# One loop over four chunks of 128 channels for the long convolution, three chunks returned through memory

## The chip, the cores and the metric

The kernel runs on one core of one Trainium2 chip. The metric is device time in microseconds of one execution; the kernel before is given by the median of three runs. A core has five engines that run their own instruction streams: TensorE (PE in the profile; its weight loads are shown apart as PEld), VectorE (DVE), ScalarE (ACT), GpSimd (POOL) and SyncE (SP). Here SP does nothing but issue transfers between the chip's memory (DRAM) and the on-chip memory.

## What is computed

A block with adaptive layer norms around two parts, for 2048 tokens of 512 channels, all in float32:

```python
mod = (silu(c) @ w_mod).reshape(6, 512)          # sa, ca, ga, sb, cb, gb
h = layernorm(q) * (1 + ca) + sa
k_shift = causal 4-tap convolution of k, per channel
kv = k_shift * v
y = causal convolution of kv with ssm_k over all 2048 tokens, per channel (by FFT)
y = y + kv * ssm_D
x = q + ga * (h * y)
h = layernorm(x) * (1 + cb) + sb
out = x + gb * ((silu(h @ w_gate) * (h @ w_up)) @ w_down)     # 512 -> 1792 -> 512
```

The kernel does the long convolution by a transform in two steps, written as matrix products: a first step of length 64 (`e_fwd`), an exchange of two axes, a second step of length 32 (`w_c`), a product with the transformed filter, and the same backwards. `ssm_D` is added to the first filter tap, so it needs no pass of its own.

## The kernel before, in words

Every engine call goes through the class `InOrder` (lines 32 to 41), which keeps each engine's instructions in the order in which the program issues them. So all rows of the profile name its line, L40, and are told apart by the tiles they write and read. Waits between engines and the places of tiles are set by the framework: a tile that asks for a place in a full pool waits until an older tile of that pool has been read for the last time.

**Places.** On-chip tiles come from pools by size: `b32` (32 KB per partition, 3 of them), `b16` (16 KB, 1), `e8` (8 KB, 9), `r4` (4 KB, 4), `k2` (2 KB, 3). Matrix products land in four pairs of PSUM banks (`banks`, line 67), handed out in turn.

**Preparing a chunk of 128 channels.** `load_k`, `load_v` and `load_ssm` bring k, v and the filter. `tap0` (line 102) and three `tap` (110) make the short convolution u on DVE (`tap0` of some chunks on ACT), `times_v` (116) multiplies by v. For the data, `trans` (146) turns four blocks of 128 x 128 for two chunks at a time on PE (tile kvt) and copies them on ACT, and `step1` (132) does the first transform step (tile s, 256 columns) with an ACT copy into X; `x1t` (157) runs both for two chunks and issues the next `trans` ahead of the two `step1`. For the filter, `skip` (512) adds `ssm_D` on DVE, `k1_step` (181) does the first step (tile s) and `k1_turn` (199) turns the result (tile kt) into K. X and K hold two chunks, 256 channels, and there are two of each (halves).

**The pieces.** The second step runs over pieces of 32 channels, 8 to a half, 16 in all. `swap` (173) exchanges the two axes of one piece of X by a 32 x 32 block transpose on DVE, in place. `k2nd(n)` (231) transforms the filter twice (`W2`, `W2S`, tile pk) and copies both results to ks on ACT; `x2nd(n)` (237) transforms the data (tile px) and multiplies px with both halves of ks on DVE, giving two R; `inv(n)` (248) turns R back (tile iv) and copies into X on ACT. `loop` (265) orders them: in step n the filter of piece n+1, the data of piece n, the swap of piece n+2, then the hooks of key `n`, `inv(n-1)`, the hooks of key `(n,)` and, in the second loop, the swap back of piece n-2.

**The order around them.** Both chunks of half 0 are prepared first (lines 516 to 562). `loop(0, 8)` (570) has the preparation of half 1's filter and u in its hooks, loads of `w_mod` (`mod_load`, 287) and the first of their products (`mod_bc`, 292, tile pb). Then comes `x1t(1)` and two more `mod_bc`. X0 isn't swapped back on DVE: `put` (210) writes it to memory, 1 KB at a time in the return by `get` (214), which reads it with the two axes exchanged, 32 partitions per transfer. The loads of the tokens (`load_x`) and of `e_inv` stand around it on SP. `loop(8, 16)` (624) has in its hooks `mod_T` (301, tile pm), the layer norm's statistics (`do_stats`, 607: DVE, with a small power on POOL), and the gates (`do_gate`, 610: two DVE and two ACT operations that scale x, then two POOL multiplications of 128 x 2048). Its last steps begin the backward first step, `y_piece` (363, tile y), which DVE multiplies into the gate S1 and `add_y` (382) adds to x.

**The entry to the feed-forward** (lines 635 to 671): the last two swaps, the split of the first weights into two parts (`split_w`, 435), the rest of y, the second layer norm of the first 512 tokens (`norm2a`, `norm2b`, `norm2c`: statistics, scale, turn on PE, split into two parts). From line 673 on `gate_up` (453, tile gu) and `down` (477, tile dn) run over 7 groups of weights and 4 groups of tokens, with three products for each float32 product.

Of the kernel before, what the change touches and what calls it, by code (L numbers as in the profile page):

```python
# [16 lines left out]
P = 128  # L17
# [26 lines left out]
def adaln_h3_swiglu(ctx, tc, q, kT, vT, shk, ssm, dskip, wgu, wdn, c, wmod, e_fwd, e_inv, w_c, out):  # L44
# [87 lines left out]
    def step1(j0, x, dst):  # L132


        ps = banks("s1")
        for jj in range(2):
            for a in range(2):
                pe.matmul(
                    ps[:, a, jj * H : (jj + 1) * H], raw[rows(a), j0 + jj], x[rows(a), jj, :], start=True, stop=True
                )  # L140
        act.copy(
            dst.rearrange("p (a j) d -> p a j d", a=2)[:, :, j0 : j0 + 2, :],
            ps.rearrange("p a (j d) -> p a j d", j=2),
        )

    def trans(h, jc):

        pt = banks("kvt")
        ptv = pt.rearrange("p a (j d) -> p (a j) d", j=2)
        for jj in range(4):  # L150
            for bb in range(2):
                pe.transpose(ptv[:, jj, bb * P : (bb + 1) * P], U[2 * h + bb][:, 4 * jc + jj :: J], ident)
        x = r4([P, 4, H], F32, f"x{h}_{jc}")
        act.copy(x, ptv)
        return x

    def x1t(h, nxt, hooks={}):
        dst = b32(f"X{h}")
        for jc in range(J // 4):
            x = nxt  # L160
            if jc + 1 < J // 4:
                nxt = trans(h, jc + 1)
            for o in range(0, 4, 2):
                step1(4 * jc + o, x[:, o : o + 2], dst)
            for f in hooks.get(jc, ()):
                f()
        return dst
# [10 lines left out]

    KT = {}

    def k1_step(h, i, jq):

        if (h, i) not in KT:
            KT[h, i] = b16(f"kt{h}{i}", (P, 4, 32, 32))
        ps = banks("s1")
        for jj in range(4):
# [72 lines left out]
    def swap_x(n):  # L259
        swap(seq[n][1], seq[n][2])  # L260
# [503 lines left out]
```

## Time and profile before

| | |
|---|---|
| runs of the kernel before | 731.72, 731.82, 733.17 us; median 731.82 |
| the profiled execution's own time | 731.3 us |
| its span, first to last instruction | 729.5 us, 8402 instructions |
| mean granted clock of TensorE | 0.954 |
| memory read and written | 40.51 and 8.39 MB |
| first product of the feed-forward (tile gu) | starts at 249.83 us |
| second step's first R, end of the last swap | 57.31 and 231.12 us |

A row of the busy times by stage gives a stretch of the span in us, its length, and for each engine its busy time in it with the number of instructions; then the granted clock of TensorE as a part of full speed, the mean busy share of the 16 transfer queues, and what they moved. The chain of waits follows the work that ended last back from the end: each row has a start, a length, an engine and the tile written; "issue" is time in which the engine waited for nothing that the profile shows. A row of the groups gives what is written and read, shapes, count, total and mean time, and the engine's idle time before it. In the list of transfers the last number is the time from issue to landing. Names without numbers stand for all tiles of that name.

### The profile page before, as it was taken

The numbers are of one execution on the slowest core, as the hardware profiler recorded it, in microseconds if no ns is written. First come the engines' busy times: TensorE is split into PE (matmuls) and PEld (weight loads), VectorE is DVE, ScalarE is ACT, GpSimd is POOL, SyncE is SP. The second block draws the span as 40 slices with busy tenths as digits, with TensorE's granted clock in tenths as the row PEclk, the third lists the DMA queues.
The fourth block names the chain that finished last, engine by engine and source line by source line (L and its number), as shares of the span: only waits on it lengthen the run. The fifth ranks groups of instructions, "written<-read, shape, count | busy, mean of one in ns | idle before, by whom it ended". The sixth has DMA issues, their size and how long they took to land.

```text
span 729.5 us, 8402 instructions
## 1 busy us (share of the span) xinstructions
PE 658.2 (90%) x3584; PEld 497.1 (68%) x3584; DVE 376.7 (52%) x476; ACT 232.9 (32%) x310; POOL 71.8 (10%) x36
## 2 busy tenths in 40 slices
PE   4499689997657679999999999999999999999997
PEld 4474345652114558888888888888888888888885
DVE  5619953269999678553334334343434433442333
ACT  3597535635312336521122112111112112211110
POOL 0000000004982353000000000000000000000000
PEclk9799989997888889999999999999999999999999
DMA  8613216996002000220000010000000000000113
GB/s 311 273 58 115 64 56 230 381 238 132 1 0 88 30 0 30 64 81 1 30 29 30 1 31 29 27 29 30 29 1 30 29 1 1 0 1 0 58 58 115
DMA packets 18150, 49.43 MB, mean 68 GB/s; under 512 B 1857, under 2 KB 6081, under 8 KB 16322
## 3 DMA queue, kind: packets, MB, share of 16 engines
q1 hardware_dynamic: 18114, 48.91, 20.2%
q8 instruction: 28, 0.46, 0.3%
q14 instruction: 8, 0.07, 0.0%
HBM read 40.51 MB, written 8.39 MB: 67 GB/s over the span
## 4 chain that ended last, share of the span: by engine, by line
PE 76%; DVE 14%; ACT 2%; DMA 2%; issue 2%; POOL 1%; SPq 0%; DVEq 0%; POOLq 0%; ACTq 0%
PE gu L40 40%; PE dn L40 21%; DVE X L40 4%; PE s L40 3%; DVE R L40 3%; PE pk L40 2%; DMA kt<-in_kT 2%; PE pb L40 2%; PE iv L40 2%; DVE s L40 1%; POOL s L40 1%; PE nt L40 1%; PE px L40 1%; PE kt L40 1%; PE kvt L40 1%
## 5 line engine op out<-in xcount | busy, mean ns | idle before, releaser
L40 PE MATMUL gu<-h,wg 128*128 128x512 f32 x1344 | 316.2, 391 | 0.4 <-DVE h L40 0.4
L40 PEld LDWEIGHTS gu<-h,wg 128*128 128x128 f32 x1344 | 253.3, 189 | 53.4 <-DVE h L40 0.8
L40 DVE TENSOR_TENSOR sg<-sg,gu 128x512 f32<-128x512 f32 x56 | 38.5, 688 | 216.7 <-ACT sg L40 216.7
L40 PE MATMUL dn<-wdb,h 128*128 128x512 f32 x576 | 138.0, 389 | 0.0
L40 ACT ACTIVATE sg<-gu 128x512 f32<-128x512 f32 x56 | 33.5, 599 | 289.2 <-PE gu L40 289.2
L40 PEld LDWEIGHTS dn<-wdb,h 128*128 128x128 f32 x576 | 108.1, 188 | 22.5
L40 DVE TENSOR_TENSOR x<-x,dn 128x512 f32<-128x512 f32 x112 | 71.9, 684 | 2.9 <-PE dn L40 2.9
L40 DVE STREAM_TRANSPOSE X<-X 128x1024 f32<-128x1024 f32 x24 | 53.5, 2249 | 36.5 <-ACT X L40 36.5
L40 DVE TENSOR_TENSOR h<-sg,h 128x512 fp32r<-128x512 f32 x56 | 38.7, 692 | 34.4 <-ACT h L40 34.4
L40 DVE TENSOR_TENSOR R<-px,ks 128x1024 f32<-128x1024 f32 x32 | 37.5, 1213 | 25.3 <-PE px L40 15.6
L40 ACT CAST h<-sg 128x512 fp32r<-128x512 f32 x56 | 34.8, 621 | 37.7 <-DVE sg L40 37.7
L40 PE MATMUL s<-er,ss 64*128 64x128 f32 x256 | 22.6, 344 | 25.5 <-issue 15.2
L40 PE MATMUL iv<-R,wc 64*64 64x512 f32 x256 | 36.7, 676 | 7.1 <-DVE R L40 3.7
L40 PE MATMUL pk<-K,wc 64*64 64x512 f32 x256 | 35.3, 675 | 7.8 <-DVE R L40 7.8
L40 PEld LDWEIGHTS s<-er,ss 64*128 64x128 f32 x256 | 20.9, 250 | 29.6 <-issue 17.0
L40 ACT COPY ks<-pk 128x1024 f32<-128x1024 f32 x32 | 31.1, 1022 | 24.4 <-PE pk L40 11.8
L40 POOL TENSOR_TENSOR s<-s,bcs 128x2048 f32<-128x2048 f32 x8 | 36.7, 4586 | 1.2 <-DVE s L40 0.9
L40 PEld LDWEIGHTS iv<-R,wc 64*64 64x64 f32 x256 | 11.3, 153 | 30.7 <-issue 23.0
L40 PE MATMUL px<-X,wc 64*64 64x512 f32 x128 | 21.0, 730 | 9.8 <-DVE R L40 9.7
L40 DVE SCALAR_TENSOR_TENSOR u<-kt,shk_sb,u 128x2047 f32<-128x2047 f32 (+2 forms) x12 | 27.9, 2327 | 2.6 <-ACT u L40 2.4
L40 ACT COPY X<-iv 128x1024 f32<-128x1024 f32 x16 | 16.2, 1010 | 32.7 <-PE iv L40 32.7
L40 PEld LDWEIGHTS pk<-K,wc 64*64 64x64 f32 x256 | 9.5, 145 | 24.2 <-issue 22.2
(68 smaller groups left out, 488.6 us busy)
## 6 DMA issues: line engine op xcount, KB each, us to landing
ws<-in_wgu SPq DMA_DIRECT2D x14, 512.0 KB, 3.3
wm<-in_wmod SPq DMA_DIRECT2D x6, 1024.0 KB, 7.7
ss<-in_ssm SPq DMA_DIRECT2D x8, 512.0 KB, 7.7
kt<-in_kT SPq DMA_DIRECT2D x4, 1024.0 KB, 7.9
vt<-in_vT SPq DMA_DIRECT2D x4, 1024.0 KB, 10.6
X<-X SPq DMA_DIRECT2D x1, 4096.0 KB, 12.4
x<-in_q SPq DMA_DIRECT2D x4, 1024.0 KB, 15.1
X<-X SPq DMA_DIRECT2D x4, 1024.0 KB, 21.4
```

Of the source, the lines that this page charges most:

```text
L40: return lambda *a, **k: self.tc.keep_in_program_order(f(*a, **k))
```

## The change

X and K now hold one chunk of 128 channels each (four of each), and one loop of 16 pieces runs over all four chunks, four pieces to a chunk. Only chunk 0 and u of chunk 1 are prepared before it. The rest of the preparation (`x_first`, `k_first`, `k_turn` and the taps, always one or two chunks ahead), the loads, the products with `w_mod`, the statistics and the gates stand in its hooks. Within a piece, the data's transform is now copied to xs (ACT), one piece ahead, and the filter's two transforms are multiplied straight out of PSUM (`product`), so that there are 16 copies of xs in place of 32 of ks. Chunks 0 to 2 go to memory and come back with the axes exchanged, in runs of 128 channels (512 bytes); chunk 3's four pieces are swapped back on DVE. The pools change: `b16` has 7 places and takes over what `b32` held, `e8` goes from 9 to 8, `r4` from 4 to 7. `load_k(0)` becomes the first large load. In the entry, `norm2b(0)` is issued before `add_y(1)`, `add_y(0)` is one operation, and `split_w(0, 2)` moves behind the first `gate_up`; the part of `w_down` for group 0 now shares its tile with the others.

```diff
-    def b32(name, shape=(P, 32, H), dt=F32):
-        return wp.tile(list(shape), dt, tag="b32", name=name, bufs=3)
-
-    def b16(name, shape, dt=F32):
-        return wp.tile(list(shape), dt, tag="b16", name=name, bufs=1)
+    def b16(name, shape=(P, 32, P), dt=F32):
+        return wp.tile(list(shape), dt, tag="b16", name=name, bufs=7)
...
-        return wp.tile(shape, dt, tag="e8", name=name, bufs=9)
+        return wp.tile(shape, dt, tag="e8", name=name, bufs=8)
...
-        return wp.tile(shape, dt, tag="r4", name=name, bufs=4)
+        return wp.tile(shape, dt, tag="r4", name=name, bufs=7)
...
+    def x_first(c_, half):
+        if half == 0:
+            X.append(b16(f"X{c_}"))
+        pt = banks("kvt").rearrange("p a (j d) -> p (a j) d", j=4)
+        for jj in range(8):
+            pe.transpose(pt[:, jj], U[c_][:, 8 * half + jj :: J], ident)
+        x = r4([P, 8, P], F32, f"x{c_}{half}")
+        act.copy(x, pt)
+        for o in range(0, 8, 4):
+            ps = banks("s1")
+            j0 = 8 * half + o
+            for jj in range(4):
+                for a in range(2):
+                    pe.matmul(
+                        ps[:, a, jj * P : (jj + 1) * P], raw[rows(a), j0 + jj], x[rows(a), o + jj], start=True, stop=True
+                    )
+            act.copy(
+                X[c_].rearrange("p (a j) d -> p a j d", a=2)[:, :, j0 : j0 + 4, :],
+                ps.rearrange("p a (j d) -> p a j d", j=4),
+            )
...
+    def put(c_):
+        away[c_] = dp.tile([P, 32, P], F32, tag=f"away{c_}", name=f"away{c_}")
+        sp.dma_start(away[c_], X[c_])
+
+    def get(c_):
+        for q_ in range(4):
+            m = away[c_][32 * q_ : 32 * q_ + 32].rearrange("p a d -> a p d")
+            sp.dma_start(X[c_][32 * q_ : 32 * q_ + 32], m)
...
-    def k2nd(n):
-        K, _, i = seq[n]
-        t = ks[n] = e8([P, 2, 2, 512], F32, "ks")
-        act.copy(t[:, 0], second(W2, K, i, "pk"))
-        act.copy(t[:, 1], second(W2S, K, i, "pk"))
-
     def x2nd(n):
-        _, X, i = seq[n]
-        px = second(W2, X, i, "px")
+        t = xs[n] = r4([P, 2, 512], F32, "xs")
+        act.copy(t, second(W2, X[n // 4], n % 4, "px"))
+
+    def product(n):
         R[n] = []
-        for g in range(2):
+        for w in (W2, W2S):
+            ps = second(w, K[n // 4], n % 4, "pk")
             r = r4([P, 2, 512], F32, "R")
-            dve.tensor_tensor(
-                r, px[:, None, g, :].to_broadcast([P, 2, 512]), ks[n][:, :, g, :], op=ALU.mult
-            )
+            dve.tensor_tensor(r, ps, xs[n], op=ALU.mult)
             R[n].append(r)
...
+    def loop(hooks):
+        for n in range(PIECES + 1):
+            if n < PIECES:
+                product(n)
+            if n + 1 < PIECES:
+                x2nd(n + 1)
+            if n + 2 < PIECES:
                 swap_x(n + 2)
             for f in hooks.get(n, ()):
                 f()
-            if n > n0:
+            if n > 0:
                 inv(n - 1)
             for f in hooks.get((n,), ()):
                 f()
-            if back and n0 + 1 < n < n1:
-                swap_x(n - 2)
...
+    load_k(0)
     load_e(0)
-    load_ssm(0, 0)
-    load_k(0)
     load_e(1)
-    load_ssm(0, 1)
+    load_ssm(0)
     load_e(2)
     load_e(3)
     load_v(0)
...
+    tap0(0, dve)
+    load_ssm(1)
+    skip(0)
+    run(kf(0, 0, 1, 2, 3))
     for t in range(1, KS):
         tap(0, t)
     times_v(0, dve)
+    x_first(0, 0)
+    x_first(0, 1)
+    run(kt(0, 0, 1, 2, 3))
+    tap0(1, dve)
     for t in range(1, KS):
         tap(1, t)
     load_k(2)
+    swap_x(0)
+    swap_x(1)
+    x2nd(0)
+    times_v(1, dve)
+    load_v(2)
+    tap0(2, act)
     skip(1)
...
+    loop({
+        0: [lambda: tap(2, 1), lambda: load_ssm(2)],
+        (0,): [lambda: x_first(1, 0), lambda: load_k(3)],
+        1: [lambda: tap(2, 2)],
+        (1,): [lambda: x_first(1, 1), lambda: load_v(3)],
+        2: [lambda: tap(2, 3)],
+        (2,): kf(1, 0, 1, 2, 3),
+        3: [lambda: times_v(2, dve), lambda: skip(2)],
+        (3,): kt(1, 0, 1, 2, 3),
+        4: [lambda: tap0(3, act), lambda: tap(3, 1)],
+        (4,): [lambda: x_first(2, 0), lambda: load_ssm(3), lambda: mod_load(1)],
+        5: [lambda: tap(3, 2)],
+        (5,): [lambda: x_first(2, 1), lambda: put(0), lambda: mod_load(2)],
+        6: [lambda: tap(3, 3)],
+        (6,): kf(2, 0, 1, 2, 3) + [lambda: mod_load(0)],
+        7: [lambda: times_v(3, dve), lambda: skip(3)],
+        (7,): kt(2, 0, 1, 2, 3) + [lambda: mod_bc(1), lambda: load_x(0), lambda: get(0)],
+        (8,): [lambda: x_first(3, 0), lambda: mod_bc(2), lambda: load_x(1)],
         9: [lambda: do_stats(0)],
+        (9,): [lambda: x_first(3, 1), lambda: mod_bc(0), lambda: put(1), lambda: load_x(2), lambda: load_x(3)],
+        10: [lambda: do_stats(1), mod_mix],
+        (10,): kf(3, 0, 1, 2, 3) + [lambda: do_gate(0), lambda: get(1), lambda: mod_load(5)],
+        11: [lambda: do_stats(2)],
+        (11,): kt(3, 0, 1, 2, 3) + [lambda: do_gate(1), load_einv],
+        12: [lambda: do_stats(3), lambda: mod_bc(5), lambda: mod_load(3)],
+        (12,): [lambda: do_gate(2), lambda: mod_load(4)],
+        (13,): [lambda: do_gate(3), lambda: put(2), lambda: mod_T(3)],
+        14: [lambda: y_now(0, 0), lambda: y_now(1, 0), lambda: swap_x(12)],
+        (14,): [lambda: mod_T(4), lambda: get(2)],
+        15: [lambda: y_now(0, 1), lambda: y_now(1, 1), lambda: swap_x(13)],
+        (16,): [lambda: swap_x(14), lambda: swap_x(15)],
+    })
     load_w(0, 0)
     load_w(0, 1)
     split_w(0, 0)
     split_w(0, 1)
     load_w(0, 2)
+    for c_ in (2, 3):
+        y_now(0, c_)
+    add_y(0, 0, 4, range(4), dve)
     rs = [norm2a(0)]
+    for c_ in (2, 3):
+        y_now(1, c_)
+    norm2b(0, rs[0])
     add_y(1, 0, 4, range(4), pool)
     norm2c(0, (0, 1))
+    for c_ in (0, 1):
+        y_now(2, c_)
     norm2c(0, (2, 3))
+    for c_ in (2, 3):
+        y_now(2, c_)
     add_y(2, 0, 4, range(4), pool)
     rs.append(norm2a(1))
...
             done = gate_up(g, t, 0)
             if g == t == 0:
                 norm2b(1, rs[1])
-                run(y01(3))
-                a = y23(3)
+                for c_ in range(4):
+                    y_now(3, c_)
...
                 add_y(3, 0, 4, range(4), pool)
+                split_w(0, 2)
```

`kf(c, ...)`, `kt(c, ...)` stand for the calls of `k_first` and `k_turn`, which do for one chunk what `k1_step` and `k1_turn` did, and `y_now(t, c)` is one chunk's part of y for 512 tokens with its DVE multiplication; `run` calls a list.

More of the change, by code (lines that the diff above doesn't have):

```diff
@@ L146, in trans @@
[L146 to L167, printed above, removed]
+                    ps[:, a, jj * P : (jj + 1) * P], SS[c_][rows(a), 4 * jq + jj], raw[rows(a), 4 * jq + jj],
@@ L523, in adaln_h3_swiglu @@
     load_v(0)
-    load_ssm(1, 0)
-    load_ssm(1, 1)
     load_k(1)
```

222 lines of the change are left out of this document (49 added, 173 removed).

## The prediction, made before the changed kernel was run

> **What bounds the kernel now.** I read the page first, then busy time by stage, then the chain of waits inside the stages. The times are of one execution of 731.3 us (span 729.5); the median of the runs is 731.82, 0.5 above it, and I take the two as equal. A repeated measurement of this kernel tells about 0.2% (1.5 us) from no change.
>
> ```profile
> PE 658.2 (90%) x3584; PEld 497.1 (68%) x3584; DVE 376.7 (52%) x476; ACT 232.9 (32%) x310; POOL 71.8 (10%) x36
> ```
>
> ```profile
> 55.00:124.00 69.00, 58.27 (x485) 30.46 (x482) 52.37 (x40) 39.73 (x48) 0.00 (x0) 0.93 0.35 123
> 124.00:149.00 25.00, 25.00 (x169) 14.57 (x168) 4.36 (x2) 18.09 (x21) 0.00 (x0) 1.00 0.82 331
> 149.00:231.00 82.00, 57.14 (x396) 23.26 (x392) 77.11 (x88) 28.19 (x31) 46.34 (x18) 0.83 0.41 86
> ...
> 281.00:729.00 448.00, 443.67 (x1971) 367.32 (x1969) 181.32 (x264) 94.97 (x144) 2.42 (x2) 1.00 0.08 29
> ```
>
> The windows give PE, weight load, DVE, ACT and POOL, then the granted clock, the share of the DMA queues and GB/s. PE's 90% hides two halves. From 281 us on, in the feed-forward part, PE is busy 443.67 of 448 us at clock 1.00, and the change touches none of that work. Everything to be had lies ahead of it, in stages with different limits: preparing two chunks (to 55), the first eight pieces (55 to 124, PE and DVE both well filled), a stretch of PE alone (124 to 149, DVE 4.36 of 25), the last eight pieces (149 to 231, DVE 77.11 of 82) and the entry to the feed-forward. PE and DVE take turns at being the bound; merging the stages can use that.
>
> ```profile
> 3.01 6.26 DMA kt<-in_kT
> ...
> 57.31 2.27 DVE R L40 x2
> ...
> 103.60 2.24 PE s L40 x32
> 105.84 3.63 PE pb L40 x8
> 109.47 1.88 PE pk L40 x16
> 111.35 0.86 PE px L40 x8
> 112.21 1.72 PE iv L40 x16
> 113.92 1.99 PE kt L40 x16
> ...
> 158.99 3.66 PE pm L40 x32
> ```
>
> These are rows of the chain of waits (start, length, what). From 103.60 on, PE's links follow one another without a gap at full clock: these are my prices.
>
> **The change part by part.** A piece costs PE its two products pk 1.88, the next px 0.86 and iv 1.72, together 4.46. Preparing a chunk on PE: `k_first` is half of the x32 row, 1.1 a call, four calls 4.4; `k_turn` half of the kt row, four calls 4.0; `x_first` eight transposes (half a kt row, 1.0), then their ACT copy, on which PE now waits because no second transpose is issued ahead, then 32 instructions of width 128 (2.1 to 2.24). For the wait I take the copy itself, priced by another of its size, and 0.1:
>
> ```profile
> L40 ACT COPY ks<-pk 128x1024 f32<-128x1024 f32 x32 | 31.1, 1022 | 24.4 <-PE pk L40 11.8 <-DVE R L40 9.9 <-DVE X L40 2.3
> ...
> L40 POOL TENSOR_TENSOR rsa<-rsa,mhalf 128x4 f32<-128x4 f32 x4 | 5.4, 1350 | 172.0 <-DVE rsa L40 171.8
> ```
>
> ```profile
> 9.37 1.29 DVE L40 TENSOR_SCALAR u<-kt,shk_sb 128x2048 f32<-128x2048 f32 x1 [2.29 <-DMA kt<-in_kT]
> 10.69 7.12 DVE L40 SCALAR_TENSOR_TENSOR u<-kt,shk_sb,u 128x2047 f32<-128x2047 f32 x3
> 17.84 2.50 DVE L40 TENSOR_TENSOR vt<-u,vt 128x512 f32<-128x512 f32 x4
> ```
>
> So an `x_first` is 4.2, two are 8.4, and a chunk's preparation 16.8, or 4.2 a piece.
>
> *Removed.* The 32 ks copies become 16 xs copies: 16 us less on ACT. Of 24 swaps 20 are left (16 forward, 4 back, since three chunks return by memory): about 9 us less on DVE. Neither counts by itself; they lower what can bound the loop. The stretch of PE alone goes into the loop. R read px and ks and now reads pk and xs, one in PSUM and one in SBUF as before, so I keep 2.27 for two; bounds -0.2 and +0.2.
>
> *Loop start.* `load_k(0)` is now first, but `skip(0)` stands on DVE behind `tap0(0)` and waits for all of `load_ssm(0)`, queued behind k and two quarters of e. Now 1.83 MB (a quarter of e 0.26, half of ssm 0.52, k 1.05) have come when k lands at 9.27; then 2.62 MB must, and 331 GB/s at a share of 0.82 makes 404: 2 us more, 11.2 (bounds 9 and 14). So the taps start where they do now (10.69): 11.2 + 7.1 + 2.5 = 20.8. Then `x_first(0)` twice, 8.4, and a last copy: X0 stands near 30, beside `tap0(1)` and its taps on DVE (20.8 + 1.3 + 7.1 = 29). Two swaps (below, 2.14 each) and `times_v(1)` (2.5): first R at **37** instead of 57.3.
>
> *Pieces 0 to 3.* DVE has R 2.27, a swap 2.14 and 2.4 of taps and `times_v` a piece, 6.9 with gaps; PE 4.46 + 4.2 = 8.7, but it has its first products ready before R starts. Laid out piece by piece that gives 31: **68**. *Pieces 4 to 7* are PE's: 4 x 8.7 + `mod_bc(1)` (3.5) = 38: **106**. *Pieces 8 and 9*: each 4.46 + 4.2 + 3.6 = 12.2: **130.5**.
>
> *Pieces 10 to 13* carry statistics and gates, as the second loop does now.
>
> ```profile
> 181.14 4.56 POOL s L40
> 185.70 0.99 DVE s L40 x2
> 186.69 2.14 DVE X L40
> 188.84 2.21 DVE R L40 x2
> 191.05 2.15 DVE X L40
> ...
> 196.63 0.91 DVE s L40 x2
> ```
>
> ```profile
> 204.01 4.09 DVE L40 TENSOR_SCALAR s<-x,rsa 128x512 f32<-128x512 f32 x2
> ```
>
> Gate to gate takes 10.9. DVE fills it (gate 0.99, two swaps 4.3, R 2.2, statistics from 193.2 to 196.6 3.4), but POOL would hold it as well: its two multiplies take 9.1, the power operation before them 1.35 and a small product, and the gate's two DVE operations start only as POOL's second multiply ends (185.70); beside POOL they took 4.09 instead of 0.99. The swap that the change takes from each of these pieces is worth nothing here: POOL is late next, at 10.7. Piece 10, ahead of POOL, has 10.1 on DVE (with `mod_mix`, two operations of the vt size, 1.3), piece 11 the 9.2 of two multiplies: 10.1 + 9.2 + 10.7 + 10.7 = 41: **171.5**.
> By the Trainium skill, SBUF — State Buffer, section Who interferes with whom, an operation that needs the port pair shared by VectorE and GpSimd blocks for the whole of the other's instruction; the 4.09 agrees, and without that rule the sum would be about 5 us lower.
>
> *Pieces 14 and 15, last swaps.* Piece 14 is PE's: 4.46, two y (1.1 each, below) and pm 3.66, 10.4. Then two y, inv, the ACT copy and the last two swaps behind R, 11.5: **193.5**, against 231.1 now.
>
> *Entry.* It goes as now (y, gate, add, statistics, scale, transposes; 231.16 to 249.83, 18.7), less what POOL's add in front of the scale costs:
>
> ```profile
> 231.16 1.12 PE y L40 x16
> ...
> 238.67 4.72 DVE n L40
> ```
>
> ```profile
> 249.83 5.73 PE L40 MATMUL gu<-h,wg 128*128 128x512 f32 x24
> ```
>
> `norm2b(0)` moves ahead of `add_y(1)`, so n should take 1.0 (the gate's price), 3.7 less; the one wide `add_y(0)` costs back 1.5. So 16.5: the first gu at **210**, 39.8 earlier. `split_w(0, 2)` leaves the path of that group: 1.2 to 1.5 us of DVE. Sum: 731.3 - 39.8 - 1.5 = **690**.
>
> *What the queue can spoil.* Each chunk returns in 512-byte pieces, half as long as now.
>
> ```profile
> 152.00:158.00 6.00, 6.00 (x44) 2.54 (x47) 2.48 (x3) 2.02 (x2) 0.00 (x0) 0.72 1.15 189
> ```
>
> ```profile
> X<-X SPq DMA_DIRECT2D x1, 4096.0 KB, 12.4
> ...
> X<-X SPq DMA_DIRECT2D x4, 1024.0 KB, 21.4
> ```
>
> Now 4.19 MB come back at 189 GB/s, 22 us. A new return of 2.10 MB costs 11 us if bytes decide and 22 if pieces do (4096 each time). The first two have over 20 us of cover. The third hasn't: with eight 8 KB buffers, `mod_load(4)` finds x0 to x3, two gates, einv and wm3 in place and waits on SP for `mod_T(3)` (near 169); `put(2)`, `get(2)` and the weights' `load_w` stand behind it. Load and put are three quarters of the put's bytes now: 9.3. The return takes 11 and 2 of latency. It lands near 191.5, just under the loop's end. I take bytes, because the 16 queues are full (1.15) at that rate.
> The Trainium skill, SBUF — State Buffer, section Door 1: The DMA port swizzle, says that partitions 0 to 31 reach 8 of the 16 ports and gives 189 GB/s for them, so its advice is to use all 128; the row agrees, and by that rule bytes decide (11 us), while by pieces the sum would be that of the first rival.
>
> **The rivals.**
> *Pieces decide (13%).* get(2) lands near 202.5, `y_now(0, 2)` stands on PE until then, and the weights that come after it push POOL's power operation: 11 later, **701**. For it: as many pieces as now; against it: full queues.
> *The stages are held back (13%).* The change doesn't do what it says: buffers or the queue delay the chunks, and all pieces run at the second loop's 10.9: 37 + 16 x 10.9 + 16.5 = 228, **708**.
> *DVE alone decides in pieces 4 to 9 (7%).* PE's copy waits get filled and the banks never bind: pieces 4 to 7 at 6.9 and 8 and 9 at 7.9 save 19, and 3 at the end: **668**. Against it: PE's links without gaps above.
> *The handshake inside a piece (5%), slower.* pk is no longer made a piece ahead, so R waits for it, and PE's next stage waits for the banks that R frees (four pairs). If PE's 8.7 and DVE's 6.9 alternate, a piece takes 15.6: 37 + 250 + 16.5 = 303, **783**. It turns the sign when the mean piece passes (249.8 + 1.5 - 37 - 16.5) / 16 = 12.4; I forecast 9.8. Against it: iv takes the R of the piece before, so PE has work behind each pk.
>
> **How the numbers follow.** The forecast, 690 (680 to 700), has 62%. The range, 676 to 712, holds it, the two late rivals, the bounds of the loop's start (-2, +3) and of R (16 x 0.2 = 3 either way); it leaves out the fastest and the slowest case, 12%. Faster 94%, within 0.2% 1%, slower 5%.
>
> **What would show it.** First R near 37; R to R 7 to 9 in pieces 0 to 7, about 12 in 8 and 9, 10 to 11 in 10 to 13 with POOL ending last; the last swap's end near 193; n at 1.0; get(2) landing 13 us after its issue with PE not waiting for it; the first gu near 210; all from 281 on the same, only earlier. A mean piece over 12, or weights of the feed-forward that arrive late, would make it wrong.

## The result and the profile after

The changed kernel takes 704.29 us (median of 701.03, 703.64, 704.94 and 705.14) against 731.77 before: ratio 0.9614 with an interval of 0.9579 to 0.9649. That is 27.5 us faster, inside the predicted range (676 to 712), and 14 us above the predicted 690; it lies outside the narrower 680 to 700, to which the prediction gave 62%. The profiled execution took 703.64, with a span of 701.8 us.

The busy line of the page and the busy time by stage, of the kernel after (columns as before):

```profile
PE 644.7 (92%) x3776; PEld 498.0 (71%) x3776; DVE 372.8 (53%) x470; ACT 216.6 (31%) x293; POOL 70.9 (10%) x36
```

```profile
37.00:70.00 33.00, 30.58 (x326) 18.05 (x328) 28.78 (x23) 20.34 (x26) 0.00 (x0) 1.00 0.35 121
70.00:108.00 38.00, 34.82 (x328) 20.73 (x324) 25.83 (x19) 24.14 (x28) 0.00 (x0) 0.96 0.57 175
108.00:130.00 22.00, 19.74 (x169) 10.48 (x162) 12.48 (x16) 10.52 (x11) 1.22 (x2) 1.00 1.10 315
130.00:172.00 42.00, 38.28 (x309) 20.93 (x311) 38.52 (x52) 22.86 (x30) 30.25 (x12) 0.94 0.47 110
172.00:195.00 23.00, 18.14 (x184) 10.06 (x176) 18.30 (x15) 4.05 (x4) 11.38 (x3) 0.95 0.94 224
195.00:215.00 20.00, 5.54 (x65) 5.03 (x65) 13.32 (x17) 3.61 (x4) 10.40 (x5) 0.67 0.37 112
...
300.00:701.00 401.00, 396.78 (x1751) 328.33 (x1749) 152.78 (x218) 73.38 (x111) 0.00 (x0) 1.00 0.06 22
```

The stretch of PE alone is gone: from 37 to 172 us PE is about 91% busy (123.42 of 135 us) with DVE beside it. One stretch stands out: from 195 to 215 us PE is busy for 5.54 of 20 us, and its granted clock is 0.67. That is the entry to the feed-forward, which the prediction had put at 16.5 us. The chain of waits of the kernel after (start, length, what) shows what it waited for:

```profile
165.61 5.49 PE pm L40 x32
171.12 0.54 SPq L40
...
171.76 11.67 DMA away<-X
183.45 0.32 SPq L40
...
185.47 13.02 DMA X<-away
...
198.62 3.33 PE y L40 x32
...
202.71 2.65 DVE x L40
...
210.33 4.73 DVE n L40
```

The chain runs through the transfers: `mod_T(3)` (pm) frees a buffer, SP issues `mod_load(4)` at 171.12 and only then `put(2)`, which lands at 183.43; the return lands at 198.49, and y(0,2) starts. Then come `add_y(0)` (x) and n, whose first operation still takes 4.73. The timelines of DVE, POOL and PE in the same kernel (start, length, what, idle time before and what ended it) give the ends:

```profile
187.40 6.38 DVE L40 STREAM_TRANSPOSE X<-X 128x1024 f32<-128x1024 f32 x3
...
210.33 5.17 DVE L40 TENSOR_SCALAR n<-x,rsb 128x512 f32<-128x512 f32 x2 [0.15 <-POOL rsb L40]
```

```profile
210.09 0.20 POOL L40 TENSOR_TENSOR rsb<-rsb 128x4 f32<-128x4 f32 x1
210.25 4.50 POOL L40 TENSOR_TENSOR x<-x,s 128x2048 f32<-128x2048 f32 x1
```

```profile
198.62 5.06 PE L40 MATMUL y<-X,ei 128*64 128x128 f32 x64 [8.48 <-DMA X<-away]
...
222.43 3.92 PE L40 MATMUL gu<-h,wg 128*128 128x512 f32 x16
```

The last swap ends at 193.78, 0.3 from the forecast. PE has been idle for 8.48 us when the return lands. `norm2b(0)` (n) is issued first on DVE, but POOL's `add_y(1)` starts 0.08 us ahead of it, and the two operations of n take 5.17 instead of 1.0. The first gu starts at 222.43, 28.65 us behind the last swap.

### The profile page after: what moved, and what is told of

It reads as the page before. It is cut to its first block, busy times and chain, and to the rows that moved or that the text cites. A ratio compares the mean times of both kernels' runs of the same rounds, so it can differ in the third digit from the quotient of the medians.

```text
span 701.8 us, 8793 instructions
## 1 busy us (share of the span) xinstructions
PE 644.7 (92%) x3776; PEld 498.0 (71%) x3776; DVE 372.8 (53%) x470; ACT 216.6 (31%) x293; POOL 70.9 (10%) x36
## 4 chain that ended last, share of the span: by engine, by line
PE 80%; DVE 9%; DMA 5%; ACT 3%; issue 2%; SPq 1%; POOL 0%; DVEq 0%; ACTq 0%
PE gu L40 42%; PE dn L40 22%; PE s L40 4%; PE pk L40 3%; PE iv L40 2%; DMA X<-away 2%; DMA away<-X 2%; PE pb L40 2%; PE px L40 1%; PE kt L40 1%; DMA ss<-in_ssm 1%; ACT x L40 1%; DVE R L40 1%; PE nt L40 1%; DVE X L40 1%
## 5 line engine op out<-in xcount | busy, mean ns | idle before, releaser
L40 PE MATMUL dn<-wdb,acts 128*128 128x512 f32 x672 | 161.5, 390 | 0.0
L40 PEld LDWEIGHTS dn<-wdb,acts 128*128 128x128 f32 x672 | 125.9, 188 | 25.9
L40 DVE TENSOR_TENSOR acts<-sg,acts 128x512 fp32r<-128x512 f32 x56 | 38.7, 692 | 34.4 <-ACT acts L40 34.4
L40 DVE TENSOR_TENSOR R<-pk,xs 128x1024 f32<-128x1024 f32 x32 | 37.6, 1215 | 29.7 <-PE pk L40 27.3
L40 ACT CAST acts<-sg 128x512 fp32r<-128x512 f32 x56 | 34.8, 621 | 37.7 <-DVE sg L40 37.7
L40 PE MATMUL s<-x,er 64*128 64x128 f32 x256 | 17.9, 294 | 9.9 <-ACT x L40 9.9
L40 ACT COPY xs<-px 128x1024 f32<-128x1024 f32 x16 | 16.2, 1012 | 30.3 <-PE px L40 28.2
L40 PE MATMUL y<-X,ei 128*64 128x128 f32 x256 | 17.5, 298 | 8.5 <-DMA X<-away 8.5
L40 PEld LDWEIGHTS y<-X,ei 128*64 128x64 f32 x256 | 16.0, 153 | 11.8 <-issue 11.0
L40 PEld LDWEIGHTS s<-x,er 64*128 64x128 f32 x256 | 16.2, 202 | 11.4 <-ACT x L40 11.4
```

What stands on the lines that cost most here:

```text
L40: return lambda *a, **k: self.tc.keep_in_program_order(f(*a, **k))
```

## The experiments

The table gives for each profiled execution the start of R(n), the end of the last swap and the start of the first gu, in us of the span, and the medians. "Entry" is the first gu less the last swap.

| kernel | R(0) | R(10) | R(14) | R(15) | last swap | first gu | entry | median |
|---|---|---|---|---|---|---|---|---|
| after | 37.03 | 132.97 | 174.56 | 183.93 | 193.78 | 222.43 | 28.65 | 704.29 |
| e1 put early | 39.59 | 135.58 | 177.28 | 190.52 | 200.92 | 222.57 | 21.65 | 703.86 |
| e2 add on DVE | 37.07 | 132.99 | 174.58 | 183.96 | 193.80 | 218.87 | 25.07 | 700.10 |
| e3 both | 38.81 | 134.77 | 176.37 | 185.75 | 195.69 | 213.91 | 18.22 | 697.66 |
| e4 gate on ACT | 37.05 | 131.38 | 172.83 | 183.44 | 193.27 | 221.33 | 28.06 | 703.04 |
| e5b e3 + turn ahead | 38.50 | 127.10 | 168.81 | 182.05 | 192.63 | 210.85 | 18.22 | 690.20 |
| e6b e2, two returns | 40.40 | 136.38 | 181.79 | 195.11 | 206.88 | 225.56 | 18.68 | 704.11 |
| e7 e3 + start order | 40.05 | 135.84 | 177.47 | 189.52 | 200.07 | 218.29 | 18.22 | 700.27 |
| e8 e3, no POOL gate | 38.69 | 134.65 | 169.02 | 181.92 | 192.44 | 210.66 | 18.22 | 690.94 |
| e9 e5b + skip late | 35.88 | 124.52 | 166.22 | 177.13 | 187.08 | 205.30 | 18.22 | 688.56 |
| e10 e5b, DVE out of POOL's way | 39.64 | 128.25 | 163.89 | 177.12 | 189.05 | 207.82 | 18.77 | 686.93 |
| e11 e9 + e10 | 36.03 | 124.67 | 159.71 | 170.71 | 180.70 | 198.93 | 18.23 | 683.27 |
| e12 e11 + wide mod_T | 35.76 | 124.39 | 164.55 | 177.38 | 187.40 | 207.24 | 19.84 | 686.69 |

The first four runs take apart the entry and one of the piece terms.

### e1: the third return issued earlier

```diff
-        (12,): [lambda: do_gate(2), lambda: mod_load(4)],
-        (13,): [lambda: do_gate(3), lambda: put(2), lambda: mod_T(3)],
+        (12,): [lambda: do_gate(2), lambda: put(2), lambda: mod_load(4)],
+        (13,): [lambda: do_gate(3), lambda: mod_T(3)],
```

> put(2) is issued on SP ahead of mod_load(4) instead of behind it; nothing else changes. Theory (the third return is on the path, and it is late because its put stands in the queue behind a load that waits for a buffer): put(2) starts near 162 instead of 171.8, get(2) has landed near 187 instead of 198.5, PE no longer waits for X before y(0,2), the first gu comes 6 to 8 us earlier, profiled time near 697. Rival (the entry's own work on DVE, ACT and POOL sets its end, and the return only happened to end there): get(2) lands earlier but the first gu moves by less than 2 us, time 702 to 704.

The median was 703.86, ratio 0.9614 (0.9595 to 0.9633): no gain, so the time is that of the rival (its four executions lie between 702.33 and 705.20). In the trace the wait went, as the theory says; SP's list, then the start of y, which now waits for the last swap and for no transfer:

```profile
161.49 0.34 SPq L40 DMA_DIRECT2D away<-X  x1
175.26 0.55 SPq L40 DMA_DIRECT2D wm<-in_wmod  x1
175.90 9.62 SPq L40 DMA_DIRECT2D X<-away  x4
```

```profile
200.97 4.51 PE L40 MATMUL y<-X,ei 128*64 128x128 f32 x48 [2.78 <-DVE X L40]
```

The entry fell from 28.65 to 21.65. What it won, the profiled execution had lost ahead of it: 2.56 us at R(0), and 3.87 between R(14) and R(15). In both places the clock was low. One window in e1:

```profile
20.00:24.00 4.00, 2.67 (x16) 2.30 (x18) 3.96 (x5) 1.01 (x1) 0.00 (x0) 0.56 0.96 354
```

and the same one in the kernel after:

```profile
20.00:24.00 4.00, 2.70 (x36) 2.54 (x37) 3.96 (x5) 1.37 (x2) 0.00 (x0) 1.00 0.96 345
```

At 0.56 PE did 16 products in the time of 36. Nothing up to 24 us differs between the two programs, so this loss at R(0) is not the edit's. For the loss in front of R(15) the run alone doesn't say that; e3 has the same edit without it (R(14) to R(15) 9.38, after: 9.37). The other three executions of e1 have no trace: that they lost their 7 us in the same way isn't shown, only that their mean granted clocks (0.965, 0.967 and 0.971) lie on the whole below those of the kernel after (0.968 to 0.974).

### e2: add_y(1) on VectorE

```diff
     norm2b(0, rs[0])
-    add_y(1, 0, 4, range(4), pool)
+    add_y(1, 0, 4, range(4), dve)
```

> add_y(1) goes to DVE behind the scale of norm2b(0) instead of to POOL. Theory (the scale n took 4.73 instead of 1.0 because POOL's add started 0.08 us ahead of it and held the port pair): n takes 1.0, the add 2.7 lies under the transposes and ACT, the first gu comes 2.5 to 4 us earlier, time near 700. Rival (n is slow by itself, or the add on DVE delays the split of h by as much as was won): n stays above 4, or the first gu moves by less than 1 us, time near 704.

Measured 700.10, ratio 0.9571 (0.9552 to 0.9591). The theory held. DVE in e2:

```profile
209.96 1.00 DVE L40 TENSOR_SCALAR n<-x,rsb 128x512 f32<-128x512 f32 x2 [0.15 <-POOL rsb L40]
210.88 2.29 DVE L40 TENSOR_TENSOR x<-x,s 128x2048 f32<-128x2048 f32 x1
```

The two operations of n take 1.00, the entry 25.07 instead of 28.65, and the loop ahead of it is the same to 0.05 us. To issue n first was not enough; POOL had to have nothing to start at that moment.

### e3: both

> Both edits together: put(2) ahead of mod_load(4), and add_y(1) on DVE. Theory (two waits that follow one another on the path): the gains add, 9 to 11 us, time near 693, and the first gu near 212. Rival (they hide one another): no more than the larger of the two, 697 or later.

Measured 697.66, ratio 0.9540 (0.9499 to 0.9582), with executions at 694.70 and 695.12 and at 700.21 and 700.36. The entry is 18.22: 10.4 less than after, and 7.0 from e1 and 3.6 from e2 make 10.6. The theory's 693 holds less well in the time: the two lower executions are 1.7 to 2.1 us above it, the median passes the rival's bound of 697. So the gains add in the trace; in the medians the two edits are worth 6.6 us, and the early put 2.4 of them over e2. The upper two executions have the lower mean clocks (0.967 and 0.971 against 0.976 and 0.977), which fits the clock as what sets them apart (last section); only one of the four has a trace.

### e4: the gate's VectorE part on ScalarE

```diff
-    def normal(dst, t, rs):
+    def normal(dst, t, rs, odd=True):
...
-            if i % 2:
+            if i % 2 and odd:
...
-        normal(lambda i: s[:, i, :], t, st1[t])
+        normal(lambda i: s[:, i, :], t, st1[t], False)
```

> The gate's two DVE operations per group go to ACT, so that DVE has no operation in pieces 10 to 13 that shares POOL's ports except the small statistics. Theory (POOL's two multiplies hold pieces 10 to 13 at 10.5 a piece through the gate's DVE operations): R to R falls to 9 to 9.5 in pieces 10 to 13, the fourteenth R comes 4 to 6 us earlier, mod_T(3), put(2) and the return come as much earlier, time near 699. Rival (DVE's own work, 9 us a piece, and PE set the pace there): R to R stays above 10, time within 1.5 us of 704.

Measured 703.04, ratio 0.9609 (0.9585 to 0.9632), the same as after; R(10) to R(14) 41.45 instead of 41.59. The theory's gain did not come; the pieces stayed above 10 us, as the rival has it. The timeline of DVE shows why:

```profile
148.31 3.75 DVE L40 TENSOR_SCALAR rsa<-mva 128x4 f32<-128x4 f32 x2
...
159.73 2.89 DVE L40 TENSOR_SCALAR rsa<-mva 128x4 f32<-128x4 f32 x2
```

These are operations on 4 elements per partition; where POOL is still they take 168 ns each (e8, next). With the gate's operations gone they are the next on DVE that meet POOL's multiplications, and they wait in their place. That explains pieces 11 and 12 (11.54 and 10.56 us). In piece 13 (10.30 us) DVE has no such operation and waits 3.73 us for TensorE:

```profile
163.80 6.98 PE L40 MATMUL pm<-csil,wm 128*128 128x1 f32 x32 [3.04 <-DVE R L40]
```

TensorE had paused for 3.04 us and ran pm at half clock (0.50 from 164 to 168 us). So two causes hide the gain in e4.

### e8: no multiplications on GpSimd

```diff
-        pool.tensor_tensor(s, s, bcs[:, None, 1, :].to_broadcast([P, 4, D]), op=ALU.mult)
-        pool.tensor_tensor(s, s, bcs[:, None, 0, :].to_broadcast([P, 4, D]), op=ALU.add)
```

> The edits of e3 stay; the gate's multiplication by and addition of the modulation rows on GpSimd, two operations of 4.6 us for each of the four token blocks, are left out (so s is the normalised input alone). It measures what GpSimd's work costs pieces 10 to 13. Theory (GpSimd's operations and the port that it shares with VectorE pace these pieces; without them VectorE's own sum, about 9 us, does): R(10) to R(14) 35 to 38 us instead of 41.6, time 691 to 694. Rival (TensorE and ScalarE pace them: the clock and the banks): R(10) to R(14) stays above 40, time 695 to 700.

This kernel leaves out what the diff removes (a multiplication and an addition, both called multiplications so far), so that s is the normalised input alone. Measured 690.94, ratio 0.9458 (0.9421 to 0.9496). R(10) to R(14) took 34.37 instead of e3's 41.60: the theory holds, and POOL's gate work costs these four pieces 7.2 us. Groups on DVE between 130 and 176 us in the kernel after (busy, mean ns of one, idle before):

```profile
L40 DVE TENSOR_SCALAR s<-x,rsa 128x512 f32<-128x512 f32 x8 | 8.8, 1140 | 0.0
...
L40 DVE TENSOR_SCALAR rsa<-mva 128x4 f32<-128x4 f32 x6 | 3.8, 673 | 0.1
```

and between 130 and 172 us in e8:

```profile
L40 DVE TENSOR_SCALAR s<-x,rsa 128x512 f32<-128x512 f32 x8 | 3.9, 533 | 0.0
...
L40 DVE TENSOR_SCALAR rsa<-mva 128x4 f32<-128x4 f32 x8 | 1.0, 168 | 0.1
```

The first group loses 4.9 us; the second, for the same six operations (three pairs of 0.24 us in e8), 3.1. That is 8.0 together, near the 7.2 from R to R, so the cost arises in DVE's waits. They are counted as busy: DVE looked full at 38.52 of the 42 us from 130 to 172 us, while some 6 us of it were waits for POOL (the rest of the 8 lies behind 172 us).

### e10: GpSimd keeps its work, VectorE is taken out of its way

On top of e5b (below): the edit of e4, and the small statistics on POOL.

```diff
-        dve.tensor_scalar(rs[:, 0, :], v, EPS, None, op0=ALU.add)
-        dve.tensor_scalar(rs[:, 1, :], m, -1.0, None, op0=ALU.mult)
+        eng = pool if name[0] == "a" else dve
+        eng.tensor_scalar(rs[:, 0, :], v, EPS, None, op0=ALU.add)
+        eng.tensor_scalar(rs[:, 1, :], m, -1.0, None, op0=ALU.mult)
```

> The edits of e5b stay (690.2). In pieces 10 to 13 VectorE is taken out of GpSimd's way: the gate's two normalising operations on VectorE go to ScalarE (as in e4), and the two small operations of the first norm's statistics (128x4), which in e4 then waited 3.75 and 2.89 us on VectorE while GpSimd multiplied, go to GpSimd itself. GpSimd's work of 9.2 us per block stays and may lag behind the pieces. Theory (VectorE's waits at the shared port, not GpSimd's own length, lengthen these pieces): R(10) to R(14) 35 to 38 us instead of 41.7, near the 34.4 of the run without GpSimd's gate, time 683 to 687. Rival (GpSimd's own 9.2 plus 1.2 us per block set the pace, since some buffer or row waits for it): R(10) to R(14) 40 or more, time 688.5 to 692.

Measured 686.93, ratio 0.9378 (0.9348 to 0.9407), as the theory has it. R(10) to R(14) took 35.64 instead of e5b's 41.71, near e8's 34.37, with all of POOL's work still done. POOL in e10:

```profile
150.69 9.20 POOL L40 TENSOR_TENSOR s<-s,bcs 128x2048 f32<-128x2048 f32 x2
...
161.74 18.28 POOL L40 TENSOR_TENSOR s<-s,bcs 128x2048 f32<-128x2048 f32 x4
```

A block takes POOL 11.05 us (150.69 to 161.74), the pieces 8.9, and POOL simply falls behind, to 180.0. So its own length does not pace the pieces. That settles what e4 left open. The edit also takes the work of these operations, about 1.2 us a piece, off DVE; what the waits alone cost is therefore read from e8, where DVE keeps that work.

### e5b: the transposes of a first stage issued ahead

On top of e3, `x_first` is cut in two: eight transposes and the copy x go ahead of `inv` of the step, the products behind it.

```diff
-        0: [lambda: tap(2, 1), lambda: load_ssm(2)],
-        (0,): [lambda: x_first(1, 0), lambda: load_k(3)],
+        0: [lambda: x_turn(1, 0), lambda: tap(2, 1), lambda: load_ssm(2)],
+        (0,): [lambda: x_mul(1, 0), lambda: load_k(3)],
...
-        (8,): [lambda: x_first(3, 0), lambda: mod_bc(2), lambda: load_x(1)],
+        8: [lambda: x_turn(3, 0)],
+        (8,): [lambda: x_mul(3, 0), lambda: mod_bc(2), lambda: load_x(1)],
```

> The edits of e3 stay (third put early, add_y(1) on VectorE: 697.66 median, profiled run 695.12 with R(0) to R(10) 95.96 us). In addition the eight transposes of each first stage in the loop and the copy behind them are issued ahead of the inverse of the piece, the raw products behind it, so that ScalarE's copy x does not wait for transposes that were issued just before it. Theory (in pieces 0 to 9 a wait between TensorE and ScalarE inside the first stage is on the path): up to 1.1 us in each of the six steps that hold a first stage, R(0) to R(10) 90 to 93 us, time 690 to 694. Rival (VectorE's own sum and the PSUM banks pace these pieces; ScalarE's wait costs nothing): R(0) to R(10) within 1 us of 95.96, time 695 to 699.

Measured 690.20, ratio 0.9435 (0.9403 to 0.9466): 7.5 us below e3. R(0) to R(10) took 88.60 instead of 95.96, more than the theory's 90 to 93 had promised. PE in step 4 of the kernel after, where the wait is longest since ACT makes `tap0(3)` in front of the copy:

```profile
71.58 1.17 PE L40 MATMUL kvt<-ident,vt 128*128 128x128 f32 x8
74.77 3.48 PE L40 MATMUL s<-x,er 64*128 64x128 f32 x32 [2.02 <-ACT x L40]
```

and in e5b:

```profile
70.64 1.17 PE L40 MATMUL kvt<-ident,vt 128*128 128x128 f32 x8
71.74 1.95 PE L40 MATMUL iv<-R,wc 64*64 64x512 f32 x16
73.62 2.06 PE L40 MATMUL s<-x,er 64*128 64x128 f32 x32
```

The inverse fills the wait. The pause of 2.02 us cost more than itself: the granted clock was 0.50 from 76 to 78 us, so the products behind it took 3.48 instead of 2.06. R(4) to R(5) went from 11.16 to 7.96.

### e6b: chunk 2 swapped back on VectorE, two returns through memory

On top of e2: `put(2)` and `get(2)` out, `swap_x(8)` to `swap_x(11)` in the hooks 11 to 14.

```diff
-        (13,): [lambda: do_gate(3), lambda: put(2), lambda: mod_T(3)],
+        (13,): [lambda: do_gate(3), lambda: mod_T(3)],
...
-        (14,): [lambda: mod_T(4), lambda: get(2)],
+        (14,): [lambda: mod_T(4)],
```

> As e2 (add_y(1) on VectorE, 700.1), but chunk 2 does not return through memory: its put and get are gone and its four swaps are done in place on VectorE, one in each of the steps 11 to 14 (2.3 us each without the shared port). This undoes one third of the return through memory. Common to both theories: no wait of TensorE for a transfer in front of y(0,2), 4 to 5 us of the entry. Theory A (VectorE and GpSimd take turns at a shared port in pieces 10 to 13, so every VectorE operation that is added lengthens the piece): R(11) to R(15) grows by 4 x 2.3 = 9.2 us or more, time 703 to 706, so the third return still pays. Theory B (GpSimd's multiplies set the length of these pieces and VectorE's part waits for them anyway): R(11) to R(15) grows by less than 4 us and the time is 696 to 700, so the third return was not worth its transfer.

Measured 704.11, ratio 0.9606 (0.9577 to 0.9635), 4 us above e2 in the median, with intervals that overlap. The entry lost 6.4 us (25.07 to 18.68), but R(11) to R(15) grew from 41.0 to 48.8 and the stretch behind R(15) from 9.8 to 11.8. The time is theory A's; the pieces don't decide. Of the growth, 3.9 us is in R(14) to R(15), where DVE waited 2.92 us for TensorE at a low clock (0.68 from 190 to 195 us). Pieces 11 and 12 grew by 2.2 and 1.6 us, nearly a swap each, as theory A has it; piece 13 by 0.1, since its swap ran while the gate would have waited for POOL, as theory B has it. The profiled execution (706.85) also lost 3.3 us ahead of R(0), which the edit doesn't touch. Without that and without the 3.9 the two kernels reach the first gu within 0.6 us of each other. So whether the third return pays is not shown.

### e7 and e9: the order of the lead-in

e7, on top of e3:

```diff
     tap0(0, dve)
     load_ssm(1)
+    tap(0, 1)
+    tap(0, 2)
     skip(0)
     run(kf(0, 0, 1, 2, 3))
-    for t in range(1, KS):
-        tap(0, t)
+    tap(0, 3)
     times_v(0, dve)
+    run(kt(0, 0, 1, 2, 3))
     x_first(0, 0)
     x_first(0, 1)
-    run(kt(0, 0, 1, 2, 3))
```

> The edits of e3 stay. In the lead-in, skip(0) and the kernel's first stage come behind the third tap instead of behind the first (VectorE waited 3.45 us for the load of ss there), and the four transposes of chunk 0's kernel spectrum come ahead of the first stage of the signal, so that TensorE has work while VectorE finishes taps and the product with v. Theory (the lead-in is VectorE's sum plus that wait; and TensorE's pauses there are what the clock drops follow): R(0) at 33.5 to 35 instead of 37.0 to 39.6, the rest shifts with it, no clock below 0.9 between 20 and 32 us, time 690 to 694 and all runs within 3 us. Rival (the loads, whose share of the DMA engines is 0.96 to 1.04 from 8 to 28 us, set the lead-in): R(0) at 36 or later, time 695 to 699.

Measured 700.27, ratio 0.9561 (0.9531 to 0.9592): 2.6 us above e3 in the median, with intervals that overlap, so no gain. R(0) came at 40.05. Neither theory had the cause. DVE and PE in e7:

```profile
33.35 4.24 DVE L40 STREAM_TRANSPOSE X<-X 128x1024 f32<-128x1024 f32 x2 [6.72 <-ACT X L40]
```

```profile
20.02 3.84 PE L40 MATMUL kt<-ident,kt 128*128 128x128 f32 x32 [1.40 <-issue]
23.70 1.07 PE L40 MATMUL kvt<-ident,vt 128*128 128x128 f32 x8
```

DVE was through the taps 3.5 us earlier, but the 3.84 us of kt that had been moved ahead (and ACT's four copies of them) put the first stage of the signal off until 23.70, and the swaps waited for it. e9 takes the first move alone, on top of e5b:

> The edits of e5b stay (690.2). Of e7's two moves only the first: skip(0) and the kernel's first stage come behind the third tap; the four transposes of the kernel spectrum stay behind the signal's first stage. In e7 VectorE ran 3.7 us earlier through the taps (tap(1) ended at 26.6 instead of 30), then waited 6.72 us for ScalarE's copies of X, which the moved transposes had pushed to 33.3. Theory (the taps were gained and the moved transposes lost them again): X is complete at 27 to 28, R(0) at 34 to 35.5 instead of 38.5, no clock below 0.9 between 20 and 32 us, time 685 to 688. Rival (the loads set the lead-in, and vT of chunk 1 comes as much later as before): R(0) at 37 or later, time 688.5 to 692.

Measured 688.56, ratio 0.9405 (0.9358 to 0.9452), with R(0) at 35.88 instead of 38.50 in e5b (the kernel after has the lead-in of e5b and came at 37.03; from 20 to 24 us its clock was 1.00, that of e5b 0.82). The swaps still waited in e9, less:

```profile
28.70 4.69 DVE L40 STREAM_TRANSPOSE X<-X 128x1024 f32<-128x1024 f32 x2 [2.18 <-ACT X L40]
```

R(0) lies 0.4 us above the theory's bound, and 1.1 below the rival's, so the loads do not set the lead-in. The time does not tell the two apart: the median lies at the rival's lower end, and its step from e5b, 1.6 us, is smaller than the scatter of the executions (685.82 to 691.53).

### e11 and e12: all of it, and another form of mod_T

e11 joins e9 and e10.

> The edits of e9 (688.56) and of e10 (686.93) together: third return early, add_y(1) on VectorE, transposes of the first stages ahead of the inverse, skip(0) behind the third tap, the gate's VectorE operations on ScalarE and the small statistics on GpSimd. Theory (the two lie in different stretches and add up): R(0) at 35.9, R(10) to R(14) 35.6, time 682 to 685. Rival (what is saved ahead is waited for behind: the loads of the mod weights, or GpSimd's backlog in front of y(3)): time 686 to 689.

Measured 683.27 (five executions), ratio 0.9315 (0.9289 to 0.9342). The two add up, as the theory says: R(0) comes at 36.03, and R(10) to R(14) takes 35.04. It is the fastest kernel of the study: 21 us below the changed kernel, 49 below the kernel before.

```diff
-        for b in range(NB):
-            for t in range(4):
-                pe.matmul(
-                    pm[:, b : b + 1], w[:, t, b * P : (b + 1) * P], csil[:, t : t + 1], start=(t == 0), stop=(t == 3)
-                )
-        dve.tensor_scalar(modT[:, i - 3, :], pm[:, 0:NB], float(i - 3), None, op0=ALU.add)
+        for t in range(4):
+            pe.matmul(pm[:, 0], csb[:, t, :], w[:, t, :], start=(t == 0), stop=(t == 3))
+        row = k2([P, D], F32, f"mr{i}")
+        act.copy(row, pm[:, 0])
+        for b in range(NB):
+            pe.transpose(pm[:, 1, b * P : (b + 1) * P], row[:, b * P : (b + 1) * P], ident)
+        dve.tensor_scalar(modT[:, i - 3, :], pm[:, 1, 0::P], float(i - 3), None, op0=ALU.add)
```

> As e11, and mod_T(3) and mod_T(4) are done in another form: instead of 32 products with one column each (in the run of e10 pm took 4.31 and 4.11 us, the granted clock fell to 0.50 from the fourth microsecond on and stayed there for 5 to 6 us, where the next sixteen pk took 3.69 us instead of 1.90), four products of 128x512 as in mod_bc (0.46 us each), one copy on ScalarE and four transposes. The numbers computed are the same. Theory (the one-column products themselves bring the clock down, since TensorE does next to nothing between weight loads): no clock below 0.9 from 150 to 185 us, R(13) to R(14) 8 to 8.5 us instead of 9.6, R(14) to R(15) 8.5 to 10 instead of 13.2, time 4 to 7 us below e11. Rival (the clock falls at this place for another reason, such as the pieces' weight loads or a pause of TensorE): clock near 0.5 again after it and the time within 2 us of e11.

Measured 686.69, ratio 0.9377 (0.9358 to 0.9395): 3.4 us slower than e11. Neither theory foresaw that. PE in e12:

```profile
153.69 3.70 PE L40 MATMUL pm<-wm,csb 128*128 128x512 f32 x8
161.45 1.12 PE L40 MATMUL pm<-ident,mr 128*128 128x128 f32 x4 [4.06 <-ACT mr L40]
162.49 3.69 PE L40 MATMUL pk<-K,wc 64*64 64x512 f32 x16
```

The products are eight in the trace, 3.70 us, not four at 0.46, so they save nothing against the 3.73 of the 32 in e11. The copy stands behind other work on ACT, TensorE pauses for 4.06 us, and the next pk ran at half clock. The edit brought a pause in, so it did not test whether the one-column products bring the clock down by themselves (more in the last section).

## Why the prediction was right, and where it was not

**What held and what didn't.** The range and the sign held. Three of the signs that the prediction had named did not: n at 1.0, a return that PE does not wait for, and the first gu near 210 (it came at 222.43).

**The loop: its sum was right.** First R at 37.03 (forecast 37); pieces 0 to 3 in 31.3 (31), 4 to 7 in 39.9 (38), 8 and 9 in 24.7 (24.5), 10 to 13 in 41.6 (41), from R(14) to the last swap 19.2 (22). The errors, +0.3, +1.9, +0.2, +0.6 and -2.8, nearly cancel: 193.78 against 193.5. That they end within 0.3 is in part luck: R(14) was 3.1 us late, and the last stretch gave 2.8 of them back. None of the four rivals came as it was described. Pieces of 11 us throughout ("held back"), "DVE alone" and the "handshake" are excluded by these lengths: the mean piece, 9.8, is the one forecast.

**Two of the loop's prices were right for a reason that was partly wrong.** For pieces 10 to 13 the text had two causes side by side: DVE, whose operations wait at the port, and "POOL is late next, at 10.7". e10 leaves POOL its work and shortens the four pieces by 6.1 us, to 8.9 us each where POOL takes 11.05, so the second cause does not hold. The first does, and it is worth 7.2 us by e8 (the prediction put it at about 5). For pieces 0 to 9 the prediction charged the ACT copy inside `x_first` to PE. That was right, and e5b shows that it was a cost of the order of issue: 7.4 us over ten pieces, with the rest of the work the same.

**The entry is the term that was mis-sized: 28.65 instead of 16.5.** The place of the late return had been named, but its size had not been seen, and two terms of the order of issue had been mis-priced.

- *The return of chunk 2 lands at 198.49 instead of 191.5.* Each link was a little short. SP got past `mod_load(4)` at 171.12 (forecast 169; pm took 5.49 instead of 3.66), load and put took 12.3 instead of 9.3, and the return 15.0 instead of 13. That makes 2.1 + 3.0 + 2.0 = 7.1. The forecast left 2 us of cover, so PE waits 4.84 us beyond the last swap; most of the rest of e1's 7.0 is y(0,2) with its gate, which e1 does ahead of that swap (197.10 us) and the kernel after behind it. The choice of bytes over pieces was right, within this: by pieces the return would have taken 22 us and 2 of latency. The first rival's place was the right one, its mechanism not.
- *n takes 5.17 instead of 1.0* (its first operation 4.73). The step "`norm2b(0)` moves ahead of `add_y(1)`, so n should take 1.0" failed. They run on different engines, and the order in the program says nothing about which starts first; both waited for the same rsb, and POOL won by 0.08 us. e2 takes POOL's operation away and has n at 1.00. The Trainium skill, SBUF — State Buffer, section Who interferes with whom, says that the order of issue decides which of the two engines blocks; these rows agree, with 0.08 us as the margin.
- *What is left, 1.7 us* (18.22 in e3). The start of n comes 9.3 us behind the last swap in e3 and 7.55 in the kernel before: 1.8 more, where the forecast charged 1.5 for the wide `add_y(0)`. From the start of n to the first gu e3 takes 8.9; the kernel before, less the forecast's 3.7, makes 7.5. That 1.4 is an order of issue that the forecast did not price. In e3, 64 products of y stand between the transposes of h and the first gu:

```profile
208.04 3.01 PE L40 MATMUL y<-X,ei 128*64 128x128 f32 x32
210.99 1.09 PE L40 MATMUL nt<-ident,n 128*128 128x128 f32 x8
212.01 1.97 PE L40 MATMUL y<-X,ei 128*64 128x128 f32 x32
```

In the kernel before there are 32, since `y01(2)` was issued ahead of the transposes, where PE waits for n anyway:

```profile
245.15 3.68 PE L40 MATMUL y<-X,ei 128*64 128x128 f32 x32
248.76 1.31 PE L40 MATMUL nt<-ident,n 128*128 128x128 f32 x8
```

The low clock behind n doesn't explain it, since the forecast's 18.7 contains it (0.50 from 243 to 249 us in the kernel before). No run moves these products back, so what that would gain isn't measured.

**The feed-forward.** `split_w(0, 2)` behind the first gu was to save 1.5 us of the first group; from the first gu to the first dn it is 30.74 instead of 31.24, so 0.5. The rest is unchanged, as forecast: in the last window PE is busy 396.78 of 401 us at full clock. With +0.3 (loop), +12.1 (entry) and +1.0 (first group), 690 becomes 703.4; the profiled execution took 703.64.

**The range held the time** because it had been drawn to take in a late third return, which gave 7.0 of the entry's 12.1 us. The 3.6 us of n and the 1.7 had no bound of their own; that the time stayed inside in spite of them is luck.

## What to carry to other kernels

A transfer whose cover is down to 2 us should be priced link by link from its issue, with what SP does ahead of it, and issued early: three of its links were each 2 to 3 us longer than forecast. VectorE's time beside a working GpSimd wasn't all VectorE's work: look in the groups for small operations with long means, and try them on another engine, as e10 does. A copy between two matrix products is free only if other TensorE work is issued between them, as e5b shows, so cut a stage in two where it waits for its own copy. The order of n and `add_y(1)` in the program did not decide which started first, since they run on two engines and waited for the same result.

## What the runs showed of the hardware

**Small operations wait as long as large ones.** VectorE operations on 128x4 elements took 168 ns each with GpSimd still (e8) and 3.75 us for two while GpSimd multiplied 128x2048 (e4).

**The clock of TensorE falls in the middle of a busy stretch, and not at the same place in every execution.** PE in e1 after a pause:

```profile
168.24 6.99 PE L40 MATMUL pm<-csil,wm 128*128 128x1 f32 x32 [3.57 <-DVE R L40]
175.16 3.69 PE L40 MATMUL pk<-K,wc 64*64 64x512 f32 x16
```

```profile
172.00:180.00 8.00, 8.00 (x40) 4.41 (x39) 7.58 (x5) 0.00 (x0) 7.49 (x3) 0.50 0.40 133
```

The pause was 3.57 us, and half clock (worked out from windows of 0.25 us, as all lengths below) lasted from 167.3 to 180.9 us, 13.7 us. In the kernel after, the same pause was 3.53 us, half clock lasted 6.8 us, from 167.3 to 174.1, and pm took 5.49 instead of 6.99. In e11 there is no pause there and pm took 3.73, but the clock fell behind it:

```profile
158.00:162.00 4.00, 4.00 (x24) 0.96 (x16) 1.90 (x2) 2.94 (x4) 3.96 (x2) 0.62 0.71 224
```

The Trainium skill, TensorE: Matmul & The Clock Gate, section What's actually happening, says that the clock is halved after an idle window of about 3.4 us, and that this window runs freely, so that its phase differs between executions. The pauses of 3.5 and 3.6 us agree, and so does the scatter: e3's executions lie in two groups 5 us apart. The lengths agree too: the stretches at half clock last 3.41 us (the kernel after from 75.1, e8 twice, e11), or about two, three or four times that (6.8 in the kernel after, 10.2 in e4, 13.7 in e1), and the starts of three of them in the kernel after, 75.14, 167.29 and 194.60, lie whole multiples of 3.41 apart. Not in that rule are falls behind shorter pauses (2.02 us in the kernel after, 3.04 in e4) and behind one-column products without a pause. Of these products the record has fifteen groups with no more than 0.4 us of pause ahead of them; behind nine of them pk took 2.46 to 3.69 us, behind six 1.95. Why it is these nine stays open: e12 was to show whether such products count as idle, and didn't.

For a comparison of kernels this means that single stages of one profiled execution can differ for no reason of the program's: R(0) lies between 37.03 and 40.40 in nine kernels with the same lead-in. Here stages were compared by their own lengths, and kernels by their medians.
